# Moving a six-element sum after each scan from VectorE to GpSimd, in a linear-attention and Fourier-mixing kernel

## The chip, the cores and the metric

The kernel runs on one core of a Trainium2 chip. The metric is device time in microseconds for one execution. The engines go by the names of the profile: PE is TensorE (PEld its weight loads), DVE is VectorE, ACT is ScalarE, POOL is GpSimd, and SP issues most of the transfers. Each engine works through its own queue in order, and waits between engines are by semaphores.

## The reference

The first block is a gated linear attention over 4 batches, 8 heads, 768 tokens and 48 channels. Its output, laid out as (4, 768, 384), is the input of a Fourier block.

```python
f = 1 / (1 + exp(-f_logit))
for t in range(S):
    state = f[t, :, None] * state + outer(k[t], v[t])
    y[t] = q[t] @ state
...
mixed = real(fft(fft(x, axis=1), axis=2))
u = x + mixed
un = (u - mean(u)) / sqrt(var(u) + 1e-6)
out = u + relu(un @ w_ch1) @ w_ch2          # 384 -> 1536 -> 384
```

## The kernel before, in words

The attention works on 16 units. Unit u is one pair of heads of batch u // 4: two heads of 48 channels lie on 112 partitions (with a gap), and the 768 tokens lie along the free dimension in six chunks of 128. The generator `attention` makes a unit, one step at each `yield`. ScalarE turns f_logit into -log f in place in the tile g (lines 411 and 444). For units 4 to 15 VectorE then scans g along the tokens into the tile W (line 449); the scan's other operand, `bound`, caps the running sum at 22 inside a chunk and at -10 at the first token of a chunk, so that every chunk starts anew. Line 450 adds, for each of the six chunks, the scan's value at the chunk's last token and the element of g one place further on, which is the next chunk's first logarithm (for the last chunk a column of zeros). The result, 112 x 6, is the unit's row T of the tile `deep`. Units 0 to 3 get their running sums from TensorE and have no such line.

After that, ScalarE overwrites g with exp(-W) and W with exp(W) (lines 453 and 454), and makes from T the decay factors `te` (line 458). VectorE multiplies g into the queries (line 462) and W with the keys (line 464). TensorE makes the scores (line 472), VectorE masks them (line 476), TensorE makes the outputs and the chunk states (lines 610 to 690, with a second scan on VectorE at line 681), ScalarE copies them out, and `fold` adds and subtracts mirrored tokens: on VectorE, and for three of four units with two copies and a subtraction on GpSimd (lines 745 to 747).

The Fourier block of a batch (`fnet`, words F; line 804 makes z with the table `tab`, lines 838 and 823 mix it with the table `cd`) and its two-layer network (`projected`, words P) come after. A network of a batch is done for pairs of chunks: `hidden` forms products of the first layer (TensorE line 925) whose sums are collected in the tile h by ScalarE (line 932) and VectorE (line 934), the second layer sums blocks of h on VectorE (lines 987 to 998, the first of them into the tile s1) and multiplies them on TensorE (line 980).

The order of the work on every engine is written out by hand: the string `ORDER` is a list of words, and each word issues one step. A bare number is the next step of that unit, so a unit's second number is its scan together with line 450, and its third is lines 453 and 454. Other words: C turns one block of weights into single precision, with the last addition on GpSimd (line 323) and the source fetched on SP by line 348; T loads the Fourier tables; S sorts them on GpSimd (lines 278 to 290: line 279 swaps two columns of `tab`, lines 282 to 290 fill `cd`); K turns a unit's keys (line 610); r fetches weights. GpSimd's queue also holds 16 indirect stores of results (line 772).

Three places of the string matter here. In the first, the second `6` is unit 6's scan, and S and the first Fourier words come behind it. In the second, a weight block (C) stands ahead of unit 7's scan (`7`, the third word after it) and another behind. In the third, units 9 and 8 issue their folds and then unit 13 its scan, its exponentials and its `te`, ahead of the next word of the network of batch 1:

```python
# "... 6 3 2 3 7 6 4 6 5 4 4 R S 3 F0 F0 ..."
# "... F0 C F0 6 7 5 5 C 6 7 ..."
# "... 9 H1 8 13 13 13 L13qv 13 P1 ..."
```

Of the kernel before, what the change touches and what calls it, by code (L numbers as in the profile page):

```python
# [10 lines left out]
ALU = mybir.AluOpType  # L11

C = 128
# [77 lines left out]
def kernel(  # L91
# [13 lines left out]
    nc = tc.nc  # L105
# [9 lines left out]
    R = 64 + D  # L115
# [19 lines left out]
    def bank(name):  # L135
        if few[0]:
            return ps_f.tile([128, 512], F32, tag="f", name=name)
        return ps_a.tile([128, 2, 512], F32, tag="sc", name=name)[:, 0]
# [12 lines left out]
    def home(name, u):  # L151

        if few[0] and u >= 2 * HP:
            u %= 2
        return {"f": g_t[u % 4], "k": k_t[u % 3], "q": q_t[u % 4]}[name]
# [247 lines left out]
    def attention(u, x_all):  # L403

        Q, K, g = home("q", u)[:R], home("k", u)[:R], home("f", u)[:R, :S]
        AT, AO = at_t[u % 2], ao_t[u % 2]
        T = deep[:R, u]  # L410
        nc.scalar.activation(g, g, AF.Exp, scale=-1.0, accum_out=hot[:R, u:u + 1])
        if u < HP:
            yield

            logs, run = early["logs"][:, u], []
            for first, n in ((0, 4), (4, 2)):  # L420
                pt = bank(f"pg{u}_{first}")
                for c in range(n):
                    nc.tensor.transpose(pt[:, c * R:(c + 1) * R], g[:, (first + c) * C:(first + c + 1) * C],
                                        ident[:R, :R])
                nc.scalar.activation(logs[:, first:first + n].rearrange("p c k -> p (c k)"), pt[:, :n * R],
                                     AF.Ln, bias=1.0)
                if first == 0:
                    yield
            yield

            sum_of = ps_a.tile([128, 2, 512], F32, tag="sc", name=f"run{u}")
            for c in range(NCH):
                nc.tensor.matmul(sum_of[:R, c // 3, c % 3 * C:c % 3 * C + C], lhsT=logs[:, c], rhs=early["upto"],
                                 start=True, stop=True)
            yield

            W = p2.tile([128, S], F32, tag="W", name=f"W{u}")[:R]
            halves = lambda a: a.rearrange("p (b n) -> p b n", b=2)
            nc.scalar.activation(halves(g), sum_of[:R, :, :3 * C], AF.Exp, scale=-1.0, bias=rise[:R])
            nc.scalar.activation(halves(W), sum_of[:R, :, :3 * C], AF.Exp, bias=low[:R])  # L440
            nc.scalar.activation(T.rearrange("p (b c) -> p b c", b=2), sum_of[:R, :, C - 1:3 * C:C], AF.Identity,
                                 bias=low[:R])
        else:
            nc.scalar.activation(g, g, AF.Ln, bias=1.0)
            yield


            W = p2.tile([128, S], F32, tag="W", name=f"W{u}")[:R]
            nc.vector.tensor_tensor_scan(W, g, bound[:R], 0.0, ALU.add, ALU.min)
            nc.vector.tensor_tensor(T, home("f", u)[:R, C::C], W[:, C - 1::C], ALU.add)  # L450
            yield

            nc.scalar.activation(g, W, AF.Exp, scale=-1.0)
            nc.scalar.activation(W, W, AF.Exp)
        yield
        te = te_t[u % 2][:R]
        ends = slice(0, NCH - 1)
        nc.scalar.activation(te[:, :, ends], T[:, ends].unsqueeze(1).to_broadcast([R, D, NCH - 1]),
                             AF.Exp, scale=-1.0, bias=low[:R])
        yield  # L460

        nc.vector.tensor_tensor(Q, Q, g, ALU.mult)
        yield
        nc.vector.tensor_tensor(g, W, K, ALU.mult)
        yield

        own = ps_a.tile([128, 2, 512], F32, tag="sc", name=f"sc{u}_0")
        for c in range(NCH):
            for s in range(2):
                o = c * C + 64 * s  # L470
                for r in range(2):
                    nc.tensor.matmul(own[64 * s:64 * s + 64, r, c * 64:c * 64 + 64], lhsT=g[ROWS[r], o:o + 64],  # L472
                                     rhs=Q[ROWS[r], o:o + 64], start=True, stop=True)
        yield

        nc.vector.copy_predicated(
            AT, causal[:, :64].bitcast(U32).unsqueeze(1).unsqueeze(1).to_broadcast([128, 2, NCH, 64]),
            own[:, :, :NCH * 64].rearrange("p r (c t) -> p r c t", t=64))
        yield
        yield from outputs(u, x_all, (AT, AO), Q, g, te)  # L480
# [591 lines left out]
    with tc.manual_schedule():  # L1072
        for word in ORDER.split():
            kind, n = word[0], int("0" + "".join(c for c in word if c.isdigit()))
            if kind.isdigit():
                if n not in units:
                    units[n] = attention(n, lambda b=n // HP: x_all(b))
# [140 lines left out]
```

## Time and profile before

| | |
|---|---|
| median of 3 runs | 512.46 us (512.06 to 513.47) |
| the profiled execution | 511.25 us, with a span of 509.5 us |
| TensorE busy | 486.2 us (95%), weight loads 450.1 us |
| VectorE busy | 373.5 us (73%), 727 instructions |
| ScalarE busy | 219.2 us (43%) |
| GpSimd busy | 84.6 us (17%), 124 instructions |

The profile is one execution. The span runs from its first to its last instruction; the execution's own time is 1.75 us more. A row of the timeline begins with the start and the duration in us, then engine, line, operation, output and inputs, and in brackets the idle time of the engine ahead of it and what ended it. A row of the windows gives, for each stretch, the busy time of PE, PEld, DVE, ACT and POOL, then the granted TensorE clock, the share of the transfer engines and GB/s. A row of the waits gives who waited for whom, us in total, how often, and the longest.

### The profile page before, as it was taken

The numbers are of one execution on the slowest core, as the hardware profiler recorded it, in microseconds if no ns is written. First come the engines' busy times: TensorE is split into PE (matmuls) and PEld (weight loads), VectorE is DVE, ScalarE is ACT, GpSimd is POOL, SyncE is SP. The second block draws the span as 40 slices with busy tenths as digits, with TensorE's granted clock in tenths as the row PEclk, the third lists the DMA queues.
The fourth block names the chain that finished last, engine by engine and source line by source line (L and its number), as shares of the span: only waits on it lengthen the run. The fifth ranks groups of instructions, "written<-read, shape, count | busy, mean of one in ns | idle before, by whom it ended". The sixth has DMA issues, their size and how long they took to land.

```text
span 509.5 us, 13793 instructions
## 1 busy us (share of the span) xinstructions
PE 486.2 (95%) x5814; PEld 450.1 (88%) x5814; DVE 373.5 (73%) x727; ACT 219.2 (43%) x528; POOL 84.6 (17%) x124
## 2 busy tenths in 40 slices
PE   5877889999999999999999999999999999999997
PEld 5766678776799999999998999999999999999997
DVE  1589999997988685687788677676777665777553
ACT  4977768855440421455434553333440413232130
POOL 4014724454231000003021000012000000010100
PEclk9999899999999999999999999999999999999999
DMA  7897764755400002013110110213101130552001
GB/s 192 234 264 185 236 190 118 233 158 155 136 0 15 19 1 62 19 41 108 37 48 32 53 50 17 69 34 100 57 0 35 61 125 17 170 174 107 33 3 38
DMA packets 20074, 46.19 MB, mean 91 GB/s; under 512 B 3489, under 2 KB 6242, under 8 KB 20002
## 3 DMA queue, kind: packets, MB, share of 16 engines
q1 hardware_dynamic: 18898, 41.66, 28.5%
q0 software_dynamic: 1104, 3.54, 1.9%
q8 instruction: 48, 0.79, 0.7%
q14 instruction: 24, 0.20, 0.1%
HBM read 40.47 MB, written 4.72 MB: 89 GB/s over the span
## 4 chain that ended last, share of the span: by engine, by line
PE 82%; DVE 2%; ACT 2%; DMA 1%; issue 1%; POOL 0%; ACTq 0%
PE ub L925 27%; PE fx L980 17%; PE fz L980 12%; PE up L957 5%; PE po L966 3%; PE z L804 3%; PE mix L823 3%; PE y L631 2%; PE y L690 2%; PE ds L673 2%; PE pt L863 2%; PE sc L472 1%; PE yt L711 1%; PE st L610 1%; DMA raw<-in_w_ch_dram 1%
## 5 line engine op out<-in xcount | busy, mean ns | idle before, releaser
L934 DVE TENSOR_TENSOR h<-h,ub 128x512 f32<-128x512 f32 x90 | 61.4, 686 | 41.0 <-PE ub L925 29.6
L932 ACT ACTIVATE h<-ub 128x512 f32<-128x512 f32 x60 | 35.4, 593 | 58.6 <-PE ub L925 56.3
L772 POOL DMA_INDIRECT out_dram<-x,place x16 | 16.4, 1023 | 227.0 <-DVE x L1038 133.1
L925 PE MATMUL ub<-wide,w 128*128 128x128 f32 x400 | 50.2, 277 | 1.6 <-DVE wide L897 1.6
L925 PEld LDWEIGHTS ub<-wide,w 128*128 128x128 f32 x400 | 47.4, 192 | 2.7 <-DVE wide L897 2.3
L937 ACT ACTIVATE h<-h 128x512 f32<-128x512 f32 x50 | 31.3, 630 | 37.7 <-DVE h L934 37.6
L980 PE MATMUL fx<-block,h 128*128 128x192 f32 x264 | 46.9, 328 | 0.0
L980 PE MATMUL fx<-w,h 128*128 128x192 f32 x264 | 45.8, 328 | 0.0
L980 PEld LDWEIGHTS fx<-block,h 128*128 128x128 f32 x264 | 43.3, 191 | 0.3
L980 PEld LDWEIGHTS fx<-w,h 128*128 128x128 f32 x264 | 42.6, 191 | 0.3
L925 PE MATMUL ub<-unT,w 128*128 128x128 f32 x320 | 41.1, 276 | 0.0
L323 POOL TENSOR_TENSOR w<-w,raw 128x384 uint32<-128x384 uint32 x24 | 30.2, 1261 | 59.6 <-ACT raw L319 39.2
L925 PEld LDWEIGHTS ub<-unT,w 128*128 128x128 f32 x320 | 38.5, 192 | 0.0
L957 PE MATMUL up<-unT,w 128*128 128x256 f32 x144 | 33.5, 385 | 0.6 <-ACT h L959 0.6
L925 PE MATMUL ub<-unT,wide 128*128 128x128 f32 x240 | 32.1, 277 | 0.0
L925 PE MATMUL ub<-wide 128*128 128x128 f32 x240 | 31.8, 276 | 0.0
L957 PEld LDWEIGHTS up<-unT,w 128*128 128x128 f32 x144 | 26.6, 190 | 5.5 <-ACT h L959 1.1
L925 PEld LDWEIGHTS ub<-unT,wide 128*128 128x128 f32 x240 | 29.3, 192 | 0.3
L925 PEld LDWEIGHTS ub<-wide 128*128 128x128 f32 x240 | 29.3, 192 | 0.0
L864 ACT COPY unT<-pt 128x384 f32<-128x384 f32 x24 | 11.5, 477 | 34.4 <-PE pt L863 34.4
L745 POOL COPY eo<-eo 128x192 f32<-128x192 f32 x12 | 6.4, 532 | 103.7 <-DVE eo L743 103.7
L980 PE MATMUL fz<-w,s 128*128 128x192 f32 x132 | 23.4, 328 | 0.0
(217 smaller groups left out, 1012.2 us busy)
## 6 DMA issues: line engine op xcount, KB each, us to landing
raw<-in_w_ch_dram SPq DMA_DIRECT2D x24, 384.0 KB, 3.9
v<-in_v_dram SPq DMA_DIRECT2D x16, 288.0 KB, 4.7
k<-in_w_ch_dram SPq DMA_DIRECT2D x12, 384.0 KB, 3.9
g<-in_w_ch_dram SPq DMA_DIRECT2D x12, 384.0 KB, 3.5
k<-in_qkf_dram SPq DMA_DIRECT2D x25, 144.0 KB, 3.6
g<-in_qkf_dram SPq DMA_DIRECT2D x20, 144.0 KB, 4.0
q<-in_qkf_dram SPq DMA_DIRECT2D x20, 144.0 KB, 3.6
wide<-in_qkf_dram SPq DMA_DIRECT2D x11, 144.0 KB, 4.2
```

The lines of the kernel that those rows point to most:

```text
L323: nc.gpsimd.tensor_tensor(bits, bits, lo, ALU.add)
L772: nc.gpsimd.indirect_dma_start(out=out.rearrange("b s d -> (b s) d"), out_offset=bass.IndirectOffsetOnAxis(ap=place[:, b, i:i + 1], axis=0 ...
L804: nc.tensor.matmul(z[:, cols], lhsT=src[:, j, lo:hi], rhs=tab[:, t, T % 2, cols], start=(i == 0), stop=(i == len(parts) - 1), skip_group_c ...
L823: nc.tensor.matmul(mix[:, o], lhsT=zz[:rows_of[T], T, PLACES[c]], rhs=cd[:rows_of[T], T, :NQ - odd], start=(i == 0), stop=(i == 1))
L864: nc.scalar.copy(turned[j][:, :, t], pt[:, :DM].rearrange("p (k t) -> p k t", k=3))
L925: nc.tensor.matmul(chains[chain][:, m * 128:(m + 1) * 128], lhsT=block(w)[:, m * 128:(m + 1) * 128], rhs=tokens(a), start=(new and m == 0) ...
L932: nc.scalar.activation(out, got, kind, scale=1.0 if how == "=+" else -1.0)
L934: nc.vector.tensor_tensor(out, out, got, ALU.add if how == "+" else ALU.subtract)
L937: nc.scalar.activation(out, out, AF.Relu)
L957: nc.tensor.matmul(pp[:, :256], lhsT=w1[:, kt, m * 128:(m + 1) * 128], rhs=unT[:, kt], start=(kt == 0), stop=(kt == 2))
L966: nc.tensor.matmul(po[:, :DM], lhsT=h[:, m, t], rhs=w2[:, m], start=(m == 0), stop=(m == NF - 1))
L980: nc.tensor.matmul(out, lhsT=h[:, m], rhs=blocks[i][:, m], start=(start and m == 0), stop=(m == H - 1), skip_group_check=True)
```

## The change

Line 450 is issued to GpSimd in place of VectorE, with the same operands. It is there for units 4 to 15, twelve times. Its place in `ORDER` stays: in GpSimd's queue it stands between what the words ahead of it and behind it issue there.

```diff
             nc.vector.tensor_tensor_scan(W, g, bound[:R], 0.0, ALU.add, ALU.min)
-            nc.vector.tensor_tensor(T, home("f", u)[:R, C::C], W[:, C - 1::C], ALU.add)
+            nc.gpsimd.tensor_tensor(T, home("f", u)[:R, C::C], W[:, C - 1::C], ALU.add)
             yield
```

## The prediction

> **What bounds the kernel now.** I read the page first, then the waits of TensorE, then the timeline of each engine around the twelve places where the changed line runs.
>
> ```profile
> span 509.5 us, 13793 instructions
> PE 486.2 (95%) x5814; PEld 450.1 (88%) x5814; DVE 373.5 (73%) x727; ACT 219.2 (43%) x528; POOL 84.6 (17%) x124
> PE 82%; DVE 2%; ACT 2%; DMA 1%; issue 1%; POOL 0%; ACTq 0%
> ...
> PE st L610 <- DVE at L476: 1.4, 1, 1.4
> ...
> PE up L957 <- ACT h L959: 0.6, 1, 0.6
> ...
> 80.00:90.00 10.00, 9.91 (x157) 8.02 (x154) 9.76 (x18) 8.29 (x23) 4.74 (x4) 1.00 0.60 170
> 200.00:300.00 100.00, 100.00 (x1198) 95.31 (x1190) 76.74 (x156) 46.05 (x110) 9.90 (x12) 1.00 0.18 54
> ```
>
> TensorE is the bound: 486.2 of 509.5 us, and 82% of the chain that ended last. After about 100 us it is full (100.00 of 100.00 in the row for 200 to 300), so any stall put into it there lengthens the run, and time given back to VectorE there is worth nothing. Between 60 and 100 us VectorE is nearly full too (9.76 of 10.00), and TensorE's two largest idle times there are the quoted 1.4 and 0.6 us. These two can absorb an early delay, and are all that an early gain could win.
>
> **What is removed.** The sums on VectorE, and what waits for them:
>
> ```profile
> L450 DVE TENSOR_TENSOR deep<-g,W x10: 168/170/803, 28.0 to 313.5; 112x6 f32<-112x6 f32 x10
> L450 DVE TENSOR_TENSOR deep<-wide,W x2: 168/484/801, 59.5 to 67.4; 112x6 f32<-112x6 f32 x2
> ...
> L450 DVE TENSOR_TENSOR deep<-g,W 112x6 f32<-112x6 f32 x10 | 3.2, 316 | 0.3
> L450 DVE TENSOR_TENSOR deep<-wide,W 112x6 f32<-112x6 f32 x2 | 1.0, 484 | 0.1
> ...
> 67.40 0.80 DVE deep L450
> ```
>
> Twelve instructions, 3.2 + 1.0 = 4.2 us of VectorE. Eight or nine cost 0.17, and by start-to-start spacing only about 0.09; the 0.80 ones stood while a GpSimd addition ran. Only one lies on the chain that ended last, the last row, so the removal alone could win 0.7 us there, if nothing else came in its place.
>
> **What is added.** The same sum on GpSimd. No row shows 112x6 there, so I bound it by its neighbours:
>
> ```profile
> 24.38 1.02 POOL L323 TENSOR_TENSOR w<-w,raw 128x384 uint32<-128x384 uint32 x1 [17.93 <-ACT raw L319]
> ...
> 47.81 0.26 POOL L746 COPY eo<-eo 1x96 f32<-1x96 f32 x1
> 48.15 1.36 POOL L747 TENSOR_TENSOR eo<-x 1x192 f32<-1x192 f32 x1
> ...
> 257.43 0.58 POOL L747 TENSOR_TENSOR eo<-x 1x192 f32<-1x192 f32 x1
> ...
> 91.94 0.85 ACT L453 ACTIVATE g<-W 112x768 f32<-112x768 f32 x1
> ```
>
> Undisturbed, 384 elements take 1.02 and 192 take 0.58: 2.3 ns each on a base of 0.14, so six take about 0.16 us (estimate). Ends: 0.1 below, 1.4 above, if it is held as the row of 1.36 is. I take 0.2. By itself that is harmless. What costs is that GpSimd works its queue in order, and ScalarE's exponential of line 453, which overwrites g, must now wait for GpSimd. So at each unit I ask what stands ahead of the sum in GpSimd's queue, and what behind it. Units 4, 5, 10, 11, 12, 14 and 15 find GpSimd idle when their scan ends; units 8 and 9 stand behind one or two weight additions, but ScalarE, busy with other work, comes to unit 8's line 453 only at 91.94, some 4 us after the sum's place, and to unit 9's later still. Cost: at most 0.1 us of ScalarE each, hidden by TensorE's own queue. If that cover were gone, seven times 0.1. Units 6, 7 and 13 remain.
>
> **Unit 6: work behind the sum.** The word S (sorting the tables) comes later in the order than unit 6's sum, but now runs before its scan:
>
> ```profile
> 54.74 0.19 POOL L278 COPY pair<-tab 128x8 f32<-128x8 f32 x1 [2.01 <-DMA tab<-in_seq_tab_dram,back]
> 55.00 0.21 POOL L279 COPY tab<-pair 128x8 f32<-128x8 f32 x1
> ...
> 61.85 1.75 POOL L290 TENSOR_SCALAR cd<-cd,half 96x192 f32<-96x192 f32 x1
> 65.84 2.34 POOL L323 TENSOR_TENSOR w<-w,raw 128x384 uint32<-128x384 uint32 x1 [2.23 <-ACT zz L811]
> ...
> 57.69 1.74 DVE L449 TENSOR_TENSOR_SCAN W<-wide,bound 112x768 f32<-112x768 f32 x1
> 59.47 0.17 DVE L450 TENSOR_TENSOR deep<-wide,W 112x6 f32<-112x6 f32 x1
> ...
> 55.64 0.84 ACT L444 ACTIVATE wide<-wide 112x768 f32<-112x768 f32 x1
> 68.24 0.84 ACT L453 ACTIVATE wide<-W 112x768 f32<-112x768 f32 x1 [0.43 <-DVE deep L450]
> 71.80 0.29 ACT L849 ACTIVATE rstd<-mv,eps 128x1 f32<-128x1 f32 x1 [1.84 <-DVE mv L846]
> 81.00 0.65 ACT L319 ACTIVATE raw<-raw,two 128x384 f32<-128x384 uint32 x1
> ...
> 68.20 0.35 SPq L348 DMA_DIRECT2D raw<-in_w_ch_dram  x1
> ...
> 58.67 1.54 PE L804 MATMUL z<-tab,se 128*95 128x385 f32 x6
> ...
> 67.15 1.50 PE L823 MATMUL mix<-cd,zz 97*128 97x193 f32 x8
> 70.08 0.70 PE L610 MATMUL st<-ident,wide 112*128 112x112 f32 x5 [1.43 <-DVE at L476]
> ```
>
> Sorting starts at 54.74 and ends at 63.60. With the sum ahead of it, GpSimd waits for the scan's end at 59.43, adds until about 59.7, and only then sorts, about 5 us later. The first z matmul reads the two sorted columns of tab. L279 ends 0.47 us after sorting begins, so at 60.2, and z starts at 60.25 instead of 58.67: TensorE loses 1.55 us. The end of the sorting moves to 59.7 + 8.86 = 68.6; the first mix, pushed by TensorE itself to 68.7, reads all of cd, so it is a tie. Ahead of st TensorE idles 1.43 us for VectorE, whose L476 now comes 0.8 earlier (the 0.09 and 0.7 of two sums), so most of the delay is swallowed: 0.1 to 0.2 us are left, and the 0.6 us wait before 98.47 takes those. Unit 7's sum stands behind the late L323: GpSimd reaches it near 69.8 to 71, so line 453 starts 1.6 to 2.9 us later than its 68.24; most of that is covered by ScalarE's idle 1.84 us ahead of its 71.80, and by what it does between there and TensorE's next need. The SP queue waits for GpSimd's L323 before it fetches raw weights at 68.20, and the loads of unit 8 stand behind; that block is not read before ScalarE's L319 at 81.00, so 2 or 3 us are hidden there. Early net: 0, with ends of -0.2 and +0.5. The gain on VectorE and the stall of TensorE cancel.
>
> How long does sorting take in its new place, beside other VectorE work? Near 48 us the copy of 0.26 ran beside VectorE's L681 scan (one input in PSUM), and the L747 of 1.36 beside the two-input L462. The Trainium skill, "SBUF — State Buffer", section "Who interferes with whom", says that a VectorE instruction with two SBUF inputs and a GpSimd one that reads SBUF fully block each other, and one with a single SBUF input does not; those two rows agree. By that rule unit 6's sum, followed on VectorE by L681, is not held; were it held for L681's 0.75 us, the sum below would be 0.3 larger.
>
> **Unit 13: work ahead of the sum.** In the order, units 9 and 8 issue their fold on GpSimd just before it.
>
> ```profile
> 254.83 1.91 POOL L747 TENSOR_TENSOR eo<-x 1x192 f32<-1x192 f32 x1
> ...
> 256.86 0.84 ACT L453 ACTIVATE g<-W 112x768 f32<-112x768 f32 x1 [2.55 <-DVE deep L450]
> 257.74 0.84 ACT L454 ACTIVATE W<-W 112x768 f32<-112x768 f32 x1
> ...
> 258.87 0.57 ACT L932 ACTIVATE h<-ub 128x512 f32<-128x512 f32 x1
> ...
> 259.48 0.96 DVE L987 TENSOR_TENSOR s<-h 128x768 f32<-128x768 f32 x1 [0.66 <-ACT h L932]
> ...
> 261.00 2.13 PE L980 MATMUL fz<-w,s 128*128 128x192 f32 x12
> ```
>
> Fold's last GpSimd instruction is the one at 257.43, quoted above; it ends at 258.01. The sum follows to 258.2, and line 453 starts at 258.25 in place of 256.86: 1.39 us late. ScalarE's queue carries that to L454, L458 and the eviction L932, for which VectorE's L987 already waits (0.66). So s1 is ready at 260.44 + 1.39 = 261.83. TensorE wants it at 261.00 for fz: it stalls 0.83, and here it is full. I take 0.9, since VectorE's work behind L987 comes late with it. Were TensorE's queue to swallow none of the lateness it would be 1.4; with VectorE earlier by the sum it no longer does, and the fold ahead running undisturbed, 0.3. If some wait further on gave it back, it would be nothing; I see none.
>
> **The sum.** 0 + 0.9 + about 0 for the rest = +0.9 us. On the profiled execution, 511.25 us (span 509.5), that is 512.15; it ran 1.2 below the median of 512.46, to which I add the same: 513.4 us.
>
> **The rivals.**
> First, both delays are hidden: fz's stall is taken in by TensorE's queue. Against it: s1 has only 0.56 us of slack. Time 512.4.
> Second, sorting runs longer than its 8.86 us, since VectorE is full from 60 to 70; L290 and L323 above show GpSimd at 1.75 and 2.34 when held by a scan. The mix starts at 59.75 + its length, against 67.15 + 1.43 + 0.55 that can be absorbed. From 10.0 us on, the loss is over 0.64 there and over 1.54 in all. At 11 us it is 1.6 + 0.9: 515.0.
> Third, the clock falls. The granted clock was 0.50 after TensorE's waits near 50 to 55 us:
>
> ```profile
> 52.00:54.00 2.00, 1.55 (x53) 1.27 (x53) 1.93 (x5) 0.23 (x1) 0.74 (x1) 1.00 0.92 304
> 56.00:58.00 2.00, 2.00 (x73) 1.88 (x67) 1.97 (x5) 1.97 (x4) 2.00 (x5) 0.50 0.83 215
> 68.00:70.00 2.00, 0.65 (x4) 0.35 (x3) 1.97 (x5) 1.69 (x2) 0.97 (x2) 1.00 1.02 236
> ```
>
> The wait of 1.43 us at 68 to 70 left it at 1.00, and the new one is about as long, which speaks against. If it fell again for the same few microseconds, about 1.7 us are lost, of which little is absorbed: 1.3 + 0.9, 514.7. The Trainium skill, "TensorE: Matmul & The Clock Gate", Part 1, puts the half clock behind an idle window of about 3.4 us; by that rule a stall of 1.55 does not do it.
> Fourth, the other side: VectorE is what holds 60 to 100 us, and three sums of 0.8 leave it there (units 7, 8, 9). If GpSimd sorted faster beside it, both quoted idle times would go, 1.43 + 0.55 = 2.0, and unit 13 would have to be hidden: 510.5. It decides only if z is not stalled, that is, if scan 6 ends before about 58; the logarithm L444 that it reads ends at 56.48, so a scan of 1.74 ends at 58.2 at the earliest.
>
> **How the numbers follow.** Forecast 0.60 (own range 512.6 to 514.0), hidden 0.10, long sorting 0.17, clock 0.06, VectorE relieved 0.07. The bound of 0.3% is 1.54 us, about what a measurement of this kernel can tell from no change: 510.92 to 514.00. Faster: 0.07. Slower: 0.17 + 0.06, and 0.02 from the forecast's tail, 0.25. Same: 0.68. The range leaves out VectorE relieved and the worst of the sorting: 511.8 to 515.1.
>
> **What would show it.** Right: GpSimd's L278 just behind a sum near 59.5; the first z near 60.2; st within 0.5 of 70.1; line 453 of unit 13 near 258.2 waiting for GpSimd, and TensorE idle about 0.8 us before fz near 261; everything after that shifted alike. Wrong: z before 59.5, st beyond 71, a clock below 1.00 after 60 us, or fz of unit 13's place without a gap.

## The result, and the profile after

| | before | after |
|---|---|---|
| median | 513.29 us (511.33 to 515.33, 20 runs) | 515.96 us (513.52 to 519.89, 20 runs) |
| profiled execution | 511.25 us, span 509.5 us | 519.26 us, span 517.5 us |

The ratio is 1.0058, with a 95% interval of 1.0038 to 1.0077: slower by 2.0 to 4.0 us, where 0.9 was forecast. The profiled execution is one of the long ones; what in it is the change and what is chance had to be found out. Its page begins so (span; busy time, share and instructions of each engine; shares of the chain that ended last):

```profile
span 517.5 us, 13800 instructions
PE 490.7 (95%) x5814; PEld 452.7 (87%) x5814; DVE 370.7 (72%) x715; ACT 219.5 (42%) x528; POOL 90.3 (17%) x136
PE 79%; DVE 4%; issue 2%; DMA 2%; POOL 1%; ACT 1%; POOLq 0%; SPq 0%; DVEq 0%; ACTq 0%
```

Twelve instructions went from VectorE (727 to 715) to GpSimd (124 to 136). TensorE has the same number of instructions and is busy 4.5 us longer, which is work at a lower clock, most of it in the windows shown below. The changed line, by its source (shortest, median, longest in ns):

```profile
L450 POOL TENSOR_TENSOR deep<-g,W x10: 193/428/1571, 29.8 to 320.1; 112x6 f32<-112x6 f32 x10
L450 POOL TENSOR_TENSOR deep<-wide,W x2: 203/203/203, 59.7 to 71.7; 112x6 f32<-112x6 f32 x2
```

Undisturbed the sum takes 0.19 to 0.20 us (0.16 was estimated, 0.2 taken); held, up to 1.57, just over the upper end of 1.4. New in TensorE's waits (us in total, times, longest) are these:

```profile
PE z L804 <- POOL tab L279: 1.4, 1, 1.4
PE sc L472 <- issue: 0.4, 1, 0.4
PE y L631 <- issue: 0.3, 1, 0.3
PE fz L980 <- DVE s L987: 0.3, 1, 0.3
```

The wait for VectorE's `at` ahead of the transposes of line 610, 1.4 us before, is gone: used up. The timeline at unit 6 (rows of GpSimd, VectorE, then TensorE):

```profile
59.65 0.20 POOL L450 TENSOR_TENSOR deep<-wide,W 112x6 f32<-112x6 f32 x1 [6.30 <-DVE W L449]
59.83 0.19 POOL L278 COPY pair<-tab 128x8 f32<-128x8 f32 x1
60.08 1.26 POOL L279 COPY tab<-pair 128x8 f32<-128x8 f32 x1
...
57.82 1.75 DVE L449 TENSOR_TENSOR_SCAN W<-wide,bound 112x768 f32<-112x768 f32 x1
60.08 0.76 DVE L681 TENSOR_TENSOR_SCAN stt<-ds,te 112x288 f32<-112x288 f32 x1 [0.50 <-PE ds L673]
60.75 0.53 DVE L763 TENSOR_TENSOR xc<-eo 128x384 f32<-128x384 f32 x1
...
61.39 2.88 PE L804 MATMUL z<-tab,se 128*95 128x385 f32 x6 [1.37 <-POOL tab L279]
72.72 1.50 PE L823 MATMUL mix<-cd,zz 97*128 97x193 f32 x8
74.06 0.64 PE L610 MATMUL st<-ident,wide 112*128 112x112 f32 x5
```

The sorting starts right behind the sum, as forecast (59.83), but the swap of two columns, line 279, takes 1.26 us where it took 0.21. The first z comes at 61.39 instead of the forecast 60.25, runs 2.88 us where it ran 1.54, and st comes 3.98 us late. The windows give the reason for the 2.88 (span; busy PE, PEld, DVE, ACT, POOL; granted clock; DMA share; GB/s):

```profile
58.00:60.00 2.00, 2.00 (x46) 1.61 (x40) 1.57 (x1) 1.27 (x4) 0.35 (x2) 0.50 0.84 238
60.00:62.00 2.00, 0.63 (x2) 0.39 (x2) 1.89 (x4) 1.57 (x2) 1.94 (x4) 0.50 1.00 332
62.00:64.00 2.00, 2.00 (x6) 1.38 (x5) 1.97 (x4) 0.00 (x0) 2.00 (x5) 0.50 0.56 191
66.00:68.00 2.00, 2.00 (x24) 1.36 (x23) 2.00 (x2) 0.98 (x5) 1.98 (x1) 0.65 0.68 183
68.00:70.00 2.00, 2.00 (x12) 1.36 (x13) 0.96 (x3) 1.60 (x10) 0.94 (x1) 1.00 0.98 230
```

The clock stood at half from 53.74 to 67.39 us; before, it was half for 3.41 us only, and back at 58.29. The timeline at unit 13:

```profile
262.24 0.58 POOL L747 TENSOR_TENSOR eo<-x 1x192 f32<-1x192 f32 x1
262.78 0.19 POOL L450 TENSOR_TENSOR deep<-g,W 112x6 f32<-112x6 f32 x1
...
263.01 0.84 ACT L453 ACTIVATE g<-W 112x768 f32<-112x768 f32 x1 [3.89 <-POOL deep L450]
...
265.63 0.96 DVE L987 TENSOR_TENSOR s<-h 128x768 f32<-128x768 f32 x1 [0.78 <-ACT h L932]
...
266.64 2.22 PE L980 MATMUL fz<-w,s 128*128 128x192 f32 x12 [0.29 <-DVE s L987]
```

This is the forecast picture, row by row: the sum just behind the fold, line 453 behind it, fz held by s. Everything stands 4.81 us later by then (the fold's subtraction of line 747 starts at 262.24 against 257.43), so line 453, at 263.01 against 256.86, is 1.34 us late of its own.

To place the loss I set the start of each matmul against that of its twin in the profile of before. The difference is +3.98 at st, +4.01 from 150 us on, +4.81 from 243.5 us on, +5.64 at fz (266.64 against 261.00) and +5.73 behind it, +5.86 at 272 us, and +6.44 from 277 us to the end. Four places, then: the stretch to 75 us, unit 13 (0.83 at fz, 0.92 with what follows it, and another 0.13 soon after), and two steps of 0.80 and 0.58 that nothing in the forecast names, the two "issue" rows above.

### The profile page after: what moved, and what is told of

The parts are those of the page before. It is cut to its first block, busy times and chain, and to the rows that moved or that the text cites. A ratio compares the mean times of both kernels' runs of the same rounds, so it can differ in the third digit from the quotient of the medians.

```text
span 517.5 us, 13800 instructions
## 1 busy us (share of the span) xinstructions
PE 490.7 (95%) x5814; PEld 452.7 (87%) x5814; DVE 370.7 (72%) x715; ACT 219.5 (42%) x528; POOL 90.3 (17%) x136
## 4 chain that ended last, share of the span: by engine, by line
PE 79%; DVE 4%; issue 2%; DMA 2%; POOL 1%; ACT 1%; POOLq 0%; SPq 0%; DVEq 0%; ACTq 0%
PE ub L925 26%; PE fx L980 16%; PE fz L980 12%; PE z L804 5%; PE up L957 4%; PE po L966 3%; PE mix L823 2%; PE y L631 2%; PE y L690 2%; PE sc L472 1%; PE pt L863 1%; PE ds L673 1%; PE yt L711 1%; DMA v<-in_v_dram 1%; DMA raw<-in_w_ch_dram 1%
## 5 line engine op out<-in xcount | busy, mean ns | idle before, releaser
L980 PE MATMUL fz<-block,h 128*128 128x192 f32 x132 | 23.3, 326 | 0.0
```

The source lines that it names most:

```text
L980: nc.tensor.matmul(out, lhsT=h[:, m], rhs=blocks[i][:, m], start=(start and m == 0), stop=(m == H - 1), skip_group_check=True)
```

## Experiments

Theory A: unit 6's late sorting and unit 13's late sum carry the loss, the first made worse by the clock. Theory B: GpSimd and VectorE get in each other's way at every sum, some 0.25 us each. Theory C: the profile's extra loss is chance. (Some expectations count ten sums in all; there are twelve.) The ratio is always to the kernel before, run in turns on the same chip, with its 95% interval.

### Units back on VectorE

`again` is the change once more. The others choose the engine by the unit:

```diff
-            nc.gpsimd.tensor_tensor(T, home("f", u)[:R, C::C], W[:, C - 1::C], ALU.add)
+            (nc.vector if u in (6,) else nc.gpsimd).tensor_tensor(T, home("f", u)[:R, C::C], W[:, C - 1::C], ALU.add)
```

with (6,) in v6, (13,) in v13, (6, 13) in v6_13.

> The changed kernel itself once more, as the measure for the others of this chip. Theory A (unit 6's late sorting stalls the first z matmul, and the stall falls into a stretch where the granted clock is already half and keeps it there; unit 13's late sum stalls fz): +2 to +3.5 us against the kernel before, z first near 60 to 61.5, clock below 0.7 somewhere between 58 and 68 us, fz of unit 13 with a gap. Theory B (twelve sums spread over the kernel get in VectorE's and GpSimd's way, about 0.25 us each): the same time, but a profile in which the lateness grows in many small steps. Theory C (the profile taken was a chance one and its low clock has nothing to do with the change): clock between 58 and 68 us at 1.00 in this profile, and the same +2 to +3.5 all the same.

> Only unit 6's sum goes back to VectorE; the other eleven stay on GpSimd. A: sorting starts near 55 again, z at about 58.7, clock 1.00 from 58.5 on; what is left is unit 13's +0.8 us against before (0.3 to 1.3). B: one twelfth is given back, so +1.9 to +3.2 us is left. C: no change of the loss beyond chance, +2 to +3.5.

> Only unit 13's sum goes back to VectorE. A: 0.8 us less than the changed kernel (about +1.2 to +2.7 against before); no idle TensorE ahead of fz near 261 to 267; the early part as in the changed kernel. B: 0.25 us less than the changed kernel. C: as B.

> Units 6 and 13 on VectorE, the other ten on GpSimd. A: nothing is left of the loss, -0.5 to +0.3 us against before. B: ten twelfths are left, +1.7 to +2.9. C: +1 to +3.

| kernel | median (before 512.87) | ratio | lateness ahead of and behind unit 13's fz, us |
|---|---|---|---|
| again | 516.59 | 1.0057 (1.0029 to 1.0086) | 3.39 to 4.32: +0.93 |
| v6 | 514.79 | 1.0038 (1.0009 to 1.0067) | -0.71 to +0.21: +0.92 |
| v13 | 514.96 | 1.0055 (1.0023 to 1.0087) | none |
| v6_13 | 514.29 | 1.0041 (1.0008 to 1.0074) | none |

Unit 13 is settled: the step is there with its sum on GpSimd, and not with it on VectorE. TensorE's wait for line 279 ahead of z is there in again (3.2 us) and, short, in v13 (0.3 us), and in neither of the other two. The times separate little: v6 (+1.9 us) and v13 (+2.8 us) lie above what theory A expected, and v6_13, where it expected about nothing, is still 2.1 us up; in its profile as in the other three stood the two unnamed steps. In again, the timeline shows how the sum itself is held:

```profile
59.83 1.08 POOL L450 TENSOR_TENSOR deep<-wide,W 112x6 f32<-112x6 f32 x1 [6.30 <-DMA vx<-in_v_dram]
...
59.67 0.73 DVE L681 TENSOR_TENSOR_SCAN stt<-ds,te 112x288 f32<-112x288 f32 x1
60.32 0.53 DVE L763 TENSOR_TENSOR xc<-eo 128x384 f32<-128x384 f32 x1
```

Here line 450 meets the scan of line 681 and ends at 60.91, 0.06 after line 763; in the first profile line 279 met it and ended at 61.34, 0.06 after line 763. An undisturbed 0.2 us would have been over before line 763 began. In this place, whichever GpSimd instruction begins within 0.3 us behind the start of that scan is held until line 763 is over.

### Single units, and the swap ahead of the sum

```diff
-            nc.gpsimd.tensor_tensor(T, ...)
+            (nc.gpsimd if u in (6,) else nc.vector).tensor_tensor(T, ...)
```

is p6; p89 has (8, 9). `split` is the change whole, with the two copies of lines 278 and 279 in a word of their own, Y, ahead of unit 6's sum:

```diff
-    "... 6 3 2 3 7 6 4 6 5 4 4 R S 3 F0 F0 ..."
+    "... 6 3 2 3 7 Y 6 4 6 5 4 4 R S 3 F0 F0 ..."
```

`twin` is the kernel before, unchanged.

> The kernel before, unchanged, profiled a second time. Five profiles of kernels with the change show two pauses of TensorE that wait for nothing the profile names, at the end of the group of line 472 of unit 12 (in the first profile of the kernel before: 238.7 us) and at the end of the group of line 631 of unit 13 (270.3 us); they move all that follows by 0.65 and 0.5 to 0.7 us. The first profile of the kernel before has neither. Theory P (the pauses belong to the changed kernels): none in this profile either, no step there against the first profile above 0.25 us. Theory C (they are chance, whether a block of instructions has come when TensorE needs it): one or both are here too, with the same 0.5 to 0.7 us. Under both the time is that of the kernel before, ratio 1.000 within 0.002.

> Only unit 6's sum is GpSimd's; the nine others are VectorE's as before. Theory A (the late sorting stalls the products of line 804 and the loss stays): line 279 copies for over 1 us instead of 0.16, the first product waits some 1.4 us for it, the forward transposes of line 610 start 1.0 to 4.0 us late depending on how long the clock stays low, no step at 260.5 us, and the time is +0.8 to +2.5 us. The prediction's theory (absorbed before line 610): that start within 0.5 us of before and the time the same. Theory R (rest in common: any of the ten sums slows the kernel some): 1.2 us more than theory A says.

> Only the sums of units 8 and 9 are GpSimd's; those of the other eight units are VectorE's as before. Theory A (units 6 and 13 carry the loss): no stall at line 804, no step at 260.5 us, the time within 0.5 us of before. Theory P (pauses of TensorE belong to the changed order): one or both steps of 0.65 us at lines 472 and 631 appear, +0.6 to +1.3 us. A gain is open: VectorE is spared two sums of 0.8 us, -0.5 us at most.

> The change whole, with the two copies of lines 278 and 279 (the swap of two columns of the table) issued ahead of unit 6's sum on GpSimd instead of behind it; the rest of the sorting stays where it was. Theory A: the products of line 804 do not wait for line 279, the early part ends within 0.5 us of before unless the clock falls by itself, unit 13's 0.9 us stay, and the time is 0.9 to 2.1 us above before, about 1 us under the change as it stands. Theory B (ten sums cost some 0.25 us each by contention): no gain over the change, +2.5 us.

| kernel | median (before 512.49) | ratio |
|---|---|---|
| twin | 512.24 | 0.9991 (0.9955 to 1.0027) |
| p6 | 514.63 | 1.0027 (0.9992 to 1.0061) |
| p89 | 510.99 | 0.9966 (0.9940 to 0.9991) |
| split | 513.47 | 1.0005 (0.9975 to 1.0036) |

p6 alone has the whole early loss, a first z at 62.13 and st at 73.63, and no step at 260.5. In split the swap is done long before the sum (lines move down by two there, so the sum is line 452):

```profile
55.99 0.41 POOL L279 COPY tab<-pair 128x8 f32<-128x8 f32 x1
58.95 1.08 POOL L452 TENSOR_TENSOR deep<-wide,W 112x6 f32<-112x6 f32 x1 [2.55 <-DVE W L451]
...
58.38 1.54 PE L806 MATMUL z<-tab,se 128*95 128x385 f32 x6
...
70.08 0.70 PE L612 MATMUL st<-ident,wide 112*128 112x112 f32 x5 [0.27 <-DVE at L478]
```

The sum is held as long as ever (1.08), but z does not wait and st starts at 70.08, to the hundredth where before has it. Two small copies in another place take most of the early loss away (0.4 to 0.6 us of it are left when measured from the scan's end, in the table below); unit 13's step of 0.92 stays. None of these four profiles had the two unnamed steps, which spoke for theory P (they belong to the changed order), though split, with all twelve sums on GpSimd, did not fit.

### Where do the two unnamed steps come from?

split13 is split with unit 13's sum on VectorE. p457 has (4, 5, 7) on GpSimd, p10_12 has (10, 11, 12). after_pad is the change with

```diff
         nc.gpsimd.memset(small, 1.0)
+        nc.gpsimd.memset(small, 1.0)
```

> As split (the swap of two columns, now lines 278 and 279 in a function of its own, issued ahead of unit 6's sum), and unit 13's sum is VectorE's again; the other eleven sums are GpSimd's. Theory A (unit 6's sorting and unit 13's late sum carry what can be traced, and the two pauses stay away as in split): no stall at line 804, no step at 260.5 us, the forward transposes within 0.5 us, and the time that of the kernel before within 0.5 us. Theory B (each sum costs some by contention): +2 us or more. VectorE is spared eleven sums of 0.2 to 0.8 us and none of it shows under either.

> Only the sums of units 4, 5 and 7 are GpSimd's. For the two pauses of TensorE at 238.7 and 270.3 us (0.5 to 0.7 us each, from 0.7 to 1.3 us after GpSimd's indirect store of line 772 began, in all five kernels that had units 4, 5, 7 to 12, 14 and 15 changed, and in none of before, twin, p6, p89 and split): theory U (the sum that stands just ahead, unit 12's, brings them): none here. Theory G (the number of instructions that stand ahead on GpSimd brings them): can't be told here, p10_12 says more. The time: within 0.5 us of before, or +1.2 us with the pauses.

> Only the sums of units 10, 11 and 12 are GpSimd's. Theory U (unit 12's sum, the last on GpSimd ahead of the pause, brings the two pauses of TensorE): both are here, +1.2 us in the profile after 238.7 us. Theory G (the place of the store of line 772 in GpSimd's stream of instructions): any of none, one or both. Theory A for the rest: no stall at line 804 and no step at 260.5 us.

> The change whole, and one more instruction on GpSimd near the start (a small memset is issued twice), so that all of GpSimd's later instructions stand one place further. Theory G: one or both pauses of TensorE at the stores of line 772 (steps of 0.65 at 238.7 and 0.5 to 0.7 at 270.3 us) are gone or stand at another store; the time is up to 1.2 us below that of the change. Theory U: both stay, and the time is that of the change, +2.7 us. The stall at line 804 and unit 13's 0.9 us stay under both.

| kernel | median (before 513.08) | ratio |
|---|---|---|
| split13 | 513.47 | 1.0009 (0.9991 to 1.0028) |
| p457 | 513.36 | 1.0017 (0.9996 to 1.0038) |
| p10_12 | 514.25 | 1.0020 (0.9997 to 1.0043) |
| after_pad | 517.23 | 1.0107 (1.0071 to 1.0143) |

All four had both steps, even p457, which has no sum on GpSimd after unit 7's near 71 us. So neither theory U nor G held, and a pattern showed: kernels profiled on one occasion all had them, or none had. The next four, on one chip, were to decide. (after_pad, of which there are six runs, is 2.5 us above again for one memset; its profile shows the losses at units 6 and 13, the two pauses, and no more. What the rest is stays open.)

twin2 is the kernel before, again2 the change, rest2 is v6_13, p89_2 is p89.

> The kernel before, unchanged, profiled on the chip on which the three kernels that follow are profiled. The two pauses of TensorE during GpSimd's stores of line 772 (steps of 0.65 at 238.7 and 0.65 at 270.3 us) were in the profiles of all nine changed kernels of three chips and in none of five of another, p6, p89 and split among them. Theory H (the pauses belong to the chip on which a kernel is profiled, not to the change): this profile has both if the three that follow have them, and neither if they have neither. Theory P (they belong to the change): this one has none whatever the others have. The time is that of before, ratio 1.000 within 0.002.

> The change whole, once more, to be held against twin2 of the same chip. Theory H with the two known losses (unit 6's late sorting, unit 13's late sum): against twin2 the start of the first product of line 804 is 1.4 to 3 us later net of what came before, unit 13 adds 0.9 to 1.0 at 260.5 us, and no step stands at 238.7 or 270.3 us; in time +1.5 to +3.3 us. Theory P: two steps of 0.65 us more against twin2.

> As v6_13: the sums of units 6 and 13 are VectorE's, the other ten GpSimd's, held against twin2 of the same chip. Theory H: its profile follows that of twin2 from 98 us to the end within 0.3 us, and its time is that of before but for what the first 70 us bring by chance and by units 4 and 5: between -0.5 and +1 us. Theory B (each sum costs some): a drift of 1 us or more between 98 us and the end.

> As p89 (only the sums of units 8 and 9 are GpSimd's), whose time was 0.9966 of before's, 0.9940 to 0.9991, with no step in its profile where these sums run. Theory D (VectorE spared two sums, a gain of 0.3 to 1.2 us): ratio 0.998 or less again. Theory E (the gain was chance in the first 35 us, where it stood in that profile): ratio 1.000 within 0.002.

| kernel | median (before 513.29) | ratio |
|---|---|---|
| twin2 | 513.16 | 0.9994 (0.9967 to 1.0022) |
| again2 | 516.29 | 1.0045 (1.0014 to 1.0076) |
| rest2 | 513.28 | 1.0011 (0.9978 to 1.0043) |
| p89_2 | 512.90 | 1.0004 (0.9972 to 1.0036) |

The timeline of twin2, the kernel before:

```profile
238.44 1.00 POOL L772 DMA_INDIRECT out_dram<-x,place  x1 [0.30 <-issue]
239.73 0.32 PE L472 MATMUL sc<-q,g 48*64 48x64 f32 x3 [0.24 <-issue]
...
270.81 1.01 POOL L772 DMA_INDIRECT out_dram<-x,place  x1 [11.59 <-DVE x L1038]
272.14 0.56 PE L673 MATMUL ds<-v,kT 128*64 128x48 f32 x14 [0.25 <-issue]
```

The kernel before has both pauses too, so they are not the change's, as theory H says. They are not the chip's either, as it also says: twin, without the pauses, and twin2 are one kernel on one chip. The first profile of before has none and the first of after has both, so 1.4 us of the difference between them (0.80 + 0.58) is that alone. Held against twin2, rest2 is 1.48 us ahead at 200 us and 1.34 at the end, so its ten sums add no more than 0.14 us there; its time agrees (1.0011), where v6_13, the same kernel, had 1.0041. p89's gain did not come back.

### The clock

before_busy and after_busy fill TensorE's idle places with small matmuls into a spare bank (word D, eight of them, 0.61 us):

```diff
-    "... 4 3 3 3 4 K5 4 6 3 2 3 7 6 4 6 5 4 4 R S 3 F0 F0 ..."
+    "... 4 3 3 3 D 4 K5 4 6 3 2 3 7 6 D 4 6 5 4 4 R S 3 D D F0 F0 ..."
```

The last two D are in after_busy only.

> The kernel before with two more words of eight small matmuls into a spare bank, where TensorE waits at about 50.4 and 55 us (in the first profile line 631 stands idle 1.02 and 1.10 us there, and the clock falls to half at 54.88 for 3.41 us). Nothing of the result depends on them. Theory K (idle TensorE ahead of 60 us is what lets the clock fall): no half clock between 45 and 75 us, mean granted clock 0.995 or more, time 0.5 to 1.5 us below before. Theory L (the clock falls there whatever TensorE does): same clock, and the time of before or up to 0.5 us above.

> The change whole with the same two words and two more behind the step that issues the sorting, where TensorE waits 1.4 us for line 279. Theory K: no half clock between 45 and 75 us, and the change loses only the delay itself and unit 13: 1.4 to 2.4 us above before_busy, mean clock 0.995 or more. Theory L: as again2 and the first profile, 2.3 to 3.3 us above before, clock 0.988 to 0.991.

| kernel | median (before 511.61) | ratio | mean clock of its runs |
|---|---|---|---|
| before_busy | 512.14 | 1.0015 (0.9985 to 1.0045) | 0.9958 |
| after_busy | 514.92 | 1.0066 (1.0034 to 1.0099) | 0.9943 |

Theory K held for the clock, or nearly (no half clock between 48 and 75 us in either profile, but a mean of 0.9943 in after_busy for the 0.995 expected), and failed for the time: before_busy is no faster, and after_busy is 2.6 us above it by the two ratios, where 1.4 to 2.4 were expected. The windows of after_busy around the stall:

```profile
60.00:62.00 2.00, 0.78 (x14) 0.60 (x11) 2.00 (x3) 0.74 (x1) 0.81 (x1) 1.00 0.89 330
62.00:64.00 2.00, 0.99 (x4) 0.67 (x5) 1.93 (x5) 1.67 (x2) 1.94 (x6) 1.00 0.96 317
```

and its timeline:

```profile
61.19 1.08 POOL L450 TENSOR_TENSOR deep<-wide,W 112x6 f32<-112x6 f32 x1 [6.31 <-DVE W L449]
62.46 0.49 POOL L279 COPY tab<-pair 128x8 f32<-128x8 f32 x1
...
63.01 1.54 PE L804 MATMUL z<-tab,se 128*95 128x385 f32 x6 [2.23 <-POOL tab L279]
72.83 0.64 PE L610 MATMUL st<-ident,wide 112*128 112x112 f32 x5
```

The clock is full although TensorE stands 2.23 us, z takes its 1.54 again, and the early loss shrinks but stays. In before_busy the first z comes earlier (58.04) and st does not (70.75): there the half clock of before is hidden behind work on other engines, and filling it wins nothing. None of the kernels is shown to be faster than the one before.

## Why the prediction was wrong

Where unit 6's scan ends differs by up to 5 us between profiles (57.70 in v6, 62.82 in again2) by what came before it, so I measure from its end. All numbers are starts and ends of rows of the timelines; a negative number means that z started first.

| kernel | scan end to first z | z to mix | mix to st | scan end to st |
|---|---|---|---|---|
| before | -0.76 | 8.48 | 2.93 | 10.65 |
| twin | 0.19 | 8.50 | 2.14 | 10.83 |
| twin2 | 0.12 | 8.48 | 2.16 | 10.76 |
| split | -0.48 | 8.81 | 2.89 | 11.22 |
| after | 1.82 | 11.33 | 1.34 | 14.49 |
| again | 1.89 | 10.18 | 1.33 | 13.40 |
| p6 | 1.90 | 10.16 | 1.34 | 13.40 |
| after_pad | 1.90 | 9.96 | 1.34 | 13.20 |
| v13 | 0.76 | 10.24 | 1.34 | 12.34 |
| again2 | 1.80 | 8.48 | 1.34 | 11.62 |
| after_busy | 1.90 | 8.48 | 1.34 | 11.72 |

**The stall of z: mis-sized.** The prediction put z 0.8 us behind the scan's end (59.43 to 60.25). In six of seven profiles it is 1.8 to 1.9; v13 alone, where the sum and line 278 were through when line 681 began, and line 279 but for 0.15 us, has the forecast 0.76. The failed step is "by that rule unit 6's sum, followed on VectorE by L681, is not held", and its price "0.3 larger": the hold was 1.0 to 1.1 us. The step looked at line 681 alone. Line 763, with two SBUF inputs, follows it at once, and it is with line 763 that the held instruction ends. GpSimd took 1.08, 1.22 or 1.26 for one instruction where 0.2 was put down, and after a held sum 0.49 for line 279. The ends of the sum, 0.1 and 1.4, did hold it; I took the low one, and of all instructions it was the one ahead of the critical copy.

The Trainium skill, "SBUF — State Buffer", "Who interferes with whom", states that a VectorE instruction with at most one SBUF input, outside its 2-port modes, does not contend with GpSimd; line 681 has one such input and the other in PSUM. By itself it held nothing here: in all twenty profiles a GpSimd copy (line 745) that begins 0.14 or 0.15 us into a later scan of line 681 takes 0.34 or 0.35 us, as it does undisturbed. Behind the scan stands line 970 there, with one input in PSUM. These rows are from before:

```profile
129.92 0.75 DVE L681 TENSOR_TENSOR_SCAN stt<-ds,te 112x288 f32<-112x288 f32 x1
130.59 0.53 DVE L970 TENSOR_TENSOR x<-po,x 128x384 f32<-128x384 f32 x1
...
130.07 0.35 POOL L745 COPY eo<-eo 128x192 f32<-128x192 f32 x1 [3.89 <-DVE eo L743]
```

So what stands behind the scan decides, although the held sums and copies would have been over 0.3 to 0.5 us before line 763 begins. Why they are held all the same stays open: behind another scan of line 681 stands line 462, also with two SBUF inputs, and there, in after_busy, a GpSimd subtraction begun 0.12 us into the scan took no more than its 0.58.

**What swallows it: right.** Mix to st fell from 2.93 to 1.34, so 1.6 us were absorbed, as forecast; in twin and twin2 there were only 0.8 to be had. At full clock the early net is therefore 11.62 and 11.72 against 10.65 to 10.83, +0.8 to +1.1, in place of the forecast 0: about the 1.1 us of the hold. (The eight other kernels with unit 6's sum on VectorE have 10.45 to 10.97.) As the wait at st was already spent, every further delay reached the end in full.

**The clock: a rival with 0.06, and it came about, in part.** In five of the seven, half clock lay on the z products, and z to mix rose by 1.5 to 2.9 us. The prediction set against it that the new wait is about as long, 1.55 us, as one that left the clock at 1.00. In after and v13 the clock was low before the wait began, from 53.74 and 53.41 us on, and the prediction had not asked for that; with the wait at the end of that stretch it stayed low in after, the extreme case with 13.65 us. In again, p6 and after_pad it stood at 1.00 and fell behind the wait, at 61.80, 62.97 and 60.56 us, for 3.41 us each. But there the wait, with the hold in it, was 3.2, 2.2 and 3.6 us. These rows are from again, the wait and the 3.41 us ahead of the fall:

```profile
PE z L804 <- POOL tab L279: 3.2, 1, 3.2
...
58.38:61.80 3.42, 0.19 (x2) 0.15 (x2) 3.35 (x6) 1.81 (x4) 1.91 (x4) 1.00 0.89 290
```

The rule used against the rival (the Trainium skill, "TensorE: Matmul & The Clock Gate", Part 1: a clock at half behind an idle window of about 3.4 us) agrees with again and after_pad, where TensorE was busy for 0.19 and 0.14 us of those 3.41, and with after_busy, 2.23 us idle at 1.00. p6 fell with 1.21 us busy. So the rule did not fail; the length of the wait that was put into it did.

What the clock cost in time is an estimate. The mean granted clock is 0.9892 in the 74 runs of the six kernels with the late sorting (after_busy left out) and 0.9912 in 180 runs of the kernel before, twin and twin2 among them; across all runs 0.01 of clock goes with about 2.3 us, so this is worth 0.5 us. But v6_13, whose sorting is early, has 0.9892 too, and the seven profiles would put it higher: their z to mix is 1.35 us longer in the mean.

**Unit 13: right.** Line 453 was forecast 1.39 late and was 1.34; the stall at fz was forecast 0.83 and was 0.83; the loss behind it was forecast 0.9 and was 0.92 or 0.93 in seven kernels (after, again, again2, v6, after_pad, split and after_busy), and none where VectorE had the sum. Another 0.12 or 0.13 follows within 6 us in all seven and in none of the others, so the whole is 1.05.

**The other ten sums: no place found.** From 98.9 us on rest2 follows the kernel before. In time v6_13 (+2.1 us), rest2 (+0.6), p457 (+0.9) and p10_12 (+1.0) all lie above it, only the first with an interval that leaves out 1; between nothing and 2 us could be in the first 70 us, where profiles of one kernel differ by as much. That stays open.

**The sum, again.** 0.8 to 1.1 (hold) + 0.5 (clock, estimated) + 1.05 (unit 13) = 2.35 to 2.65 us, against 2.3 to 3.0 from the ratios of after, again and again2. The forecast had 0 + 0.9. The hold and unit 13 are shown by kernels with and without them; that the rest closes is not shown, since v6_13 has neither loss and is 2.1 us up (0.4 to 3.8), and after_busy has no half clock on z and is 2.6 us above before_busy. Long sorting, the prediction's largest rival, did not decide: the mix was pushed by TensorE itself (72.72, sorting over at 68.94). VectorE's relief showed nowhere: split and split13 have it, without most of the early loss, and are no faster than before.

The two unnamed pauses (1.4 us) stand in the comparison of the first two profiles but not in the change, and would have been blamed on it without a second profile of the kernel before.

## What to carry to other kernels

When a small instruction moves to another queue, the price is what stands behind it there: list who reads the results of the next few instructions in that queue, and time the move with the moved instruction at the upper end of its price, not at its undisturbed one. Look also at what the other engine does right behind the instruction that runs beside it: here line 763, not line 681, set when the sum was over. A slack can be spent once; ask how much of it the same kernel has in a second profile (0.8 or 1.6 us here) before a delay is booked against it. If a queue must take the instruction, issue the one urgent piece behind it first: two copies put ahead of the sum gave back most of the early loss.

## What was not expected of the hardware

TensorE paused in two dense groups of small matmuls beside GpSimd's indirect store (line 772). The idle time in the rows, 0.17 to 0.46 us, ends 1.2 to 1.3 us after the store's start, and what follows comes 0.5 to 0.9 us later than in profiles without the pause. The work and its phase are the same there (sc of unit 12 starts 0.04 us after the store in split, which has no pause, and in again, which has it). All kernels profiled on one occasion had it, or none, twin and twin2 on the same chip included; what makes the occasion is open.

Half clock came in stretches of 3.41 us or a multiple (3.41, 6.83, 10.24, 13.65), at places that changed from profile to profile of one kernel: 15.62 and 53.16 us in twin2, 54.88 in before. In the twenty profiles the clock fell 27 times ahead of 75 us, and each time TensorE had been busy for 4% to 60% of the 3.41 us just before. Not every stretch as thin brought a fall: in after_busy TensorE was busy for 1.47 us of 61.07 to 64.48 and the clock stayed at 1.00.

A GpSimd copy of 8 elements or a sum of 6, issued while VectorE runs the scan of line 681 and then, without a gap, the addition of line 763 with two SBUF inputs, ends 0.05 to 0.06 us after that addition (after, again, again2, after_busy), 0.9 to 1.05 us late. The hold lasts over several VectorE instructions if there is no gap between them: unit 5's sum in after began 0.15 us behind line 462, took 1.57 us and ended 0.06 us after the third of three instructions with two SBUF inputs (lines 462, 739 and 740). In again line 739 began 0.02 us after line 462 was over, and the sum took 0.84.
